# Attention and two gated layers on one core: where the reciprocals and the keys' load stand in a half

## The chip, the cores and the metric

The kernel runs on one core of a Trainium2 chip. The metric is the device time of one launch in microseconds (us); lower is better. A core has five engines that run their own instruction streams: PE (TensorE, matmuls), DVE (VectorE), ACT (ScalarE), POOL (GpSimd) and SP (SyncE, which here only issues DMAs). Each takes its instructions in program order and waits on semaphores.

## The reference

Attention over 4 batches and 8 heads of 1152 tokens with 64 channels, the queries averaged in pairs of tokens, and then two gated layers on the 2304 resulting rows of 512.

```python
q_pool = q.reshape(B, H, S // 2, 2, D).mean(axis=3)
scores = np.matmul(q_pool, k.transpose(0, 1, 3, 2)) / np.sqrt(D)
scores = scores - np.max(scores, axis=-1, keepdims=True)
attn = np.exp(scores)
attn = attn / (np.sum(attn, axis=-1, keepdims=True) + 1e-09)
x = np.matmul(attn, v)            # -> (B*S/2, H*D) rows
h = x @ w_in;  x = (h - np.tanh(h)) @ w_out
h = x @ w2_in; x = (h / (1 + np.exp(-1.702 * h))) @ w2_out
```

## The kernel before

Heads are handled in 16 pairs, `p` = 0 to 15, the two heads of a pair on the two halves of the partitions. The 576 pooled queries of a pair are cut in two, so the attention stage is a loop of 32 halves, `h` = 2p + x. [...]

A half does, for nine blocks of 128 keys, the scores (`scores`, line 429 on PE: three products and one with `row`, which subtracts the row maximum), the exponent on ScalarE (line 435), and sums of the exponents on GpSimd (line 446) and VectorE (line 464). In between, `unit` (lines 351, 359, 366) computes the plain scores of the next pair for its row maxima, which VectorE reduces (line 371). `send_rows` (lines 380 to 391) transposes the maxima on VectorE and sends them into `row` by small DMAs of SyncE: six in the odd half (part 0, before the next pair's scores start) and four in the even one (part 1; `end_rows`, line 394, finishes them). At the end of a half `products` multiplies the exponents by the values (line 480, 72 matmuls) and adds up the denominators (line 493); ScalarE copies the result out (line 501).

The order within a half is written by hand. Jobs are filed under a half and a place with `at(h, place, fn)` and run by `do(h, place)`. The places, in order: "first" and "start" (ahead of the loop over blocks and units), then after the loop "load", "pre", "gp", then `products`, then "end" and "pool". Within one place jobs run in the order in which they were filed; the weight pieces of the first gated layer are filed before the attention's own jobs.

The steps that matter here, for pair p with h = 2p:

- `sums(p - 1)`, line 514, at the start of half h: four small DMAs on SyncE bring the denominators of the previous pair into `s9`.
- `recip(p - 1)`, lines 522, 523 and 525, at the end of half h (for the last but one half at "pre"): VectorE adds three columns and takes the reciprocal `r9`, SyncE sends it to the DRAM tile `rd` (4.6 KB).
- `spread(p - 1)`, line 531, at the start of half h + 1: two DMAs on SyncE read `rd` back, broadcast over 64 partitions each, into `rbd`. They wait until `rd` has landed.
- `normalise(p - 1)`, line 540, at the end of half h + 1: VectorE multiplies the result by `rbd`.
- `load_k(p)`, line 290, at "first" of half h - 4: SyncE loads the keys into one of two buffers `kr`, whose last reader is `prep_kl` of pair p - 2 on GpSimd, at the end of half h - 5.
- `load_v(p)` (line 294, half h - 2) and `load_sum(p)` (line 285, half h - 4) at "load"; `fetch_low` (line 342) at "first" of half h - 1: further loads on SyncE.
- `load_other(p)`, line 281, at "gp" of half h - 6, and `take_qh(p)`, line 338, at "gp" of half h - 3: GpSimd issues DMAs that add to a DRAM tile, on a queue of their own.
- `prep_kh(p)`, line 321, at "pre" of half h - 3: ScalarE rounds the keys. `prep_kl(p)`, line 328, at "pool": GpSimd takes the low part; a dependency set by hand (`after`, with `last["v"]`) holds it until the VectorE instruction that `last["v"]` names is done. In an even half that was the reciprocal, in an odd one `normalise`.
- The weight pieces' conversion (`convert_steps`, lines 143, 149, 156, 163 on VectorE) runs one step in each half from half 2 on, mostly at "end", ahead of `recip`.

Of the kernel before, what the change touches and what calls it, by code (L numbers as in the profile page):

```python
# [23 lines left out]
def f32(ap):  # L24
    return ap.bitcast(F32)
# [3 lines left out]
def tile_pooled_attention_two_moe(  # L29
# [11 lines left out]
    nc = tc.nc  # L41
# [85 lines left out]
    last = {}  # L127

    def after(job, first):
        if first is not None:  # L130
            tc.add_manual_dep(job.ins, first.ins.name, mybir.DependencyInfo(
                mybir.DependencyClass.Sync, mybir.DependencyReason.DATA), reason="port")

    def convert_steps(raw, hi, lo, shape, box, eng=None):
        def shift():
            box["t"] = wpool.tile([128, DM], I32, tag="wt", name="wt", bufs=2)
            if raw.dtype == F32:
                nc.scalar.activation(f32(box["t"][:]), raw, AF.Copy)
                return
            top = raw[:, :, 1]  # L140
            box["a"] = wpool.tile([128, DM], F32, tag="wa", name="wa", bufs=1)
            nc.scalar.activation(box["a"], f32(top), AF.Abs)
            nc.vector.tensor_scalar(  # L143
                out=box["t"], in0=top, scalar1=3, scalar2=0x3FFFFFF8,
                op0=ALU.logical_shift_left, op1=ALU.bitwise_and,
            )

        def sign():
            nc.vector.scalar_tensor_tensor(  # L149
                out=box["t"], in0=raw[:, :, 1], scalar=-0x40000000, in1=box["t"],  # L150
                op0=ALU.bitwise_and, op1=ALU.bitwise_or,
            )

        def flush():
            t, a = box["t"], box["a"]
            nc.vector.scalar_tensor_tensor(
                out=f32(t[:]), in0=a, scalar=2.0 ** -15 * 1.125, in1=f32(t[:]),
                op0=ALU.is_ge, op1=ALU.mult,
            )

        def tail():
            t = box["t"]
            nc.vector.scalar_tensor_tensor(
                out=t, in0=raw[:, :, 0], scalar=29, in1=t,
                op0=ALU.logical_shift_right, op1=ALU.bitwise_or,
            )

        def split():
            t = f32(box["t"][:]).rearrange("p (a b) -> p a b", a=shape)
            nc.scalar.activation(hi, t, AF.Copy)  # L170
            job = (eng or nc.gpsimd).tensor_tensor(lo, t, f32(hi), op=ALU.subtract)  # L171
            if eng is None:
                after(job, last.pop("rest", None))

        def nothing():
            pass

        bits = [sign, flush, tail] if raw.dtype == I32 else [nothing] * 3
        return [shift, *bits, split]

# [38 lines left out]
    def attention(ctx: ExitStack):  # L219
# [19 lines left out]
        rows = [ap.tile([128, SP], F32R, name=f"row{i}") for i in range(2)]  # L239
# [152 lines left out]
        def end_rows(p):  # L392
            d = pairs[p]
            nc.vector.tensor_reduce(
                d["row"][:, 512:], f32(d["cr"][:]).rearrange("p (h i) -> p i h", h=2),
                AX.X, ALU.min)
# [17 lines left out]
        def scores(g, some=slice(0, 4)):  # L414
            p, i = divmod(g, 2 * KT)
            x, t = divmod(i, KT)
            d = pairs[p]
            sc = opened.pop(g, None)
            if sc is None:
                sc = ps.tile([128, 2, 512], F32, tag="ps", name="sc")  # L420
            else:
                some = slice(3, 4)
            ks, xs = slice(128 * t, 128 * t + 128), slice(HB * x, HB * x + HB)
            steps = (
                (d["kh"][:, ks], d["qh"]), (d["kl"][:, ks], d["qh"]),
                (d["kh"][:, ks], d["ql"]), (sel, d["row"]))
            for n, (w, m) in list(enumerate(steps))[some]:
                for s, r in enumerate(sides):
                    nc.tensor.matmul(  # L429
                        sc[:, s, 0:HB], w[r], m[r, xs], start=(n == 0), stop=(n == 3))  # L430
            if some.stop < 4:
                opened[g] = sc
                return
            pf = ap.tile([128, 2, HB], F32, tag="pf", name="pf", bufs=10)
            nc.scalar.activation(pf, sc[:, :, 0:HB], AF.Exp, scale=SCALE)  # L435
            probs[g] = pf
# [13 lines left out]
        def full(p, x):  # L450
            return 1 < 2 * p + x < 2 * NPAIR - 1

        def rest_of(p, x):
            return ((5, 6, 7, 8),) if full(p, x) else ((5, 6), (7, 8))
# [13 lines left out]
        def add_two(p, x, t):  # L468
            two = [probs[(2 * p + x) * KT + i] for i in (t - 1, t)]
            pairs[p]["twos"].append(ap.tile([128, 2, HB], F32, tag=f"two{t}", name="two"))  # L470
            nc.vector.tensor_add(pairs[p]["twos"][-1], *two)
# [74 lines left out]
        def at(h, when, fn, *args):  # L546
            jobs.setdefault((h, when), []).append(lambda: fn(*args))

        def do(h, when):
            for job in jobs.pop((h, when), ()):  # L550
                job()
# [3 lines left out]
        NH = 2 * NPAIR  # L555
# [32 lines left out]
        for p in range(NPAIR):  # L588
            h = 2 * p
            if p > 0:  # L590
                at(h - 2, "load", load_v, p)
                if p == 1:
                    at(h - 2, "pre", prep_corner, p)
                    at(h - 2, "end", prep_ql, p)
                    at(h - 2, "pool", prep_kl, p, 0)
                    at(h - 1, "end", prep_kl, p, 1, nc.vector)
                else:
                    at(h - 2, "pool", prep_kl, p, 0)
                    at(h - 1, "pool", prep_kl, p, 1)
                    at(h - 1, "first", fetch_low, p, "ql")  # L600
                at(h, "start", sums, p - 1)
                at(h, "pre" if h == NH - 2 else "end", recip, p - 1)
                at(h + 1, "start", spread, p - 1)
                at(h + 1, "end", normalise, p - 1)
            if p > 1:
                at(h - 4, "start", new_pair, p)
                at(max(h - 6, 0), "start", load_one, p)
                at(max(h - 6, 0), "gp" if p > 2 else "start", load_other, p)
                at(h - 4, "load", load_sum, p)
                at(h - 4, "first", load_k, p)  # L610
                at(h - 3, "pre", prep_qh, p)
                at(h - 3, "pre", prep_corner, p)
                at(h - 3, "pre", minus_qh, p)
                at(h - 3, "pre", prep_kh, p, 0)
                at(h - 3, "pre", prep_kh, p, 1)
                at(h - 3, "gp", take_qh, p)
# [13 lines left out]
        first, second = slice(0, 128), (slice(128, 2 * 128), slice(2 * 128, 3 * 128))  # L630
# [37 lines left out]
        for h in range(NH):  # L668
            p, x = divmod(h, 2)
            do(h, "first")  # L670
            do(h, "start")
            g = h * KT
            t = 0
            late = [t for g in rest_of(p, x) for t in g[1:]] if h < NH - 1 else []
            for u in todo[h]:
                if u is None:
                    scores(g + t)
                    if h < NH - 1 and t < KADD - full(p, x) or t < 4:
                        add(p, x, t)
                    elif h == NH - 1 and t in (5, 7):  # L680
                        add_two(p, x, t)
                    t += 1
                    if t == KT and late and h != 1:
                        add_rest(p, x, late.pop(0))
                    continue
                unit(*u)
                if u == (p + 1, 6):
                    max_rows(p + 1, 0)
                    send_rows(p + 1, 0)
                if u == (p, 10):  # L690
                    max_rows(p, 1)
                    send_rows(p, 1)
                if t == KT and late:
                    add_rest(p, x, late.pop(0))
                    if late and x == 0 and full(p, x):
                        add_rest(p, x, late.pop(0))
                        end_rows(p)
            while late:
                add_rest(p, x, late.pop(0))
            if h == NH - 2:  # L700
                end_rows(p)
            do(h, "load")
            do(h, "pre")
            do(h, "gp")
            products(p, x)
            if x == 0 and not full(p, x):
                end_rows(p)
            do(h, "end")
            do(h, "pool")
# [652 lines left out]
```

## Time and profile before

| | us |
|---|---|
| median of 3 runs | 1172.92 |
| lowest and highest | 1171.52, 1174.12 |
| the profiled execution | 1176.05 |
| its span, first to last instruction | 1174.3 |
| attention stage, about | 0 to 395 |
| PE busy in the span | 1161.6 (99%) |
| DVE, ACT, POOL busy | 992.5, 652.9, 453.6 |
| DMA moved | 156.29 MB |

The page gives the share of the span in which each engine had an instruction at work. PE's matmuls are pipelined and their ends are modelled, so its 99% says that it hardly ever stood still, not that it was at its peak. The granted clock of PE is listed per stretch; 1.00 is full speed, 2.4 GHz, and 0.50 is 1.2 GHz. A DMA's issue is a SyncE instruction of some 0.3 to 0.6 us; its landing comes later and is known through those who wait for it.

### The profile page before, as it was taken

How to read it: one execution, taken by the hardware profiler on the slowest of the kernel's cores; microseconds unless marked ns; L12 is line 12 of the kernel's file. 1: busy time of each engine (PE TensorE's matmuls, PEld its weight loads, DVE VectorE, ACT ScalarE, POOL GpSimd, SP SyncE). 2: the span in 40 equal slices, each digit the busy share in tenths (PEclk: the TensorE clock that was granted, in tenths of full speed). 3: DMA queues.
4: the chain of work that ended last, by engine and by line, in shares of the span. 5: the costliest groups of instructions: out<-in, count | busy, mean ns of one | idle time of the engine just before them, and what ended most of it. 6: DMA issues, size and time to landing. Idle time of an engine off the chain costs nothing.

```text
span 1174.3 us, 23203 instructions
## 1 busy us (share of the span) xinstructions
PE 1161.6 (99%) x9260; PEld 971.5 (83%) x9260; DVE 992.5 (85%) x1242; ACT 652.9 (56%) x969; POOL 453.6 (39%) x321
## 2 busy tenths in 40 slices
PE   9999999999999999999999999999999999999998
PEld 7767676767777888888898898898889999999996
DVE  6888988878988799999999999998986899886442
ACT  4667566656665678676666666655654333342220
POOL 7667676766766223333232333221000222222211
PEclk9999999999999999999999999999999999999999
DMA  6455655555542021111111111112998757765512
GB/s 191 123 118 137 162 127 133 146 143 130 125 111 62 12 64 36 55 54 37 54 36 54 37 36 36 37 54 95 389 389 311 275 215 287 269 225 206 206 54 90
DMA packets 58221, 156.29 MB, mean 133 GB/s; under 512 B 14080, under 2 KB 19712, under 8 KB 58112
## 3 DMA queue, kind: packets, MB, share of 16 engines
q1 hardware_dynamic: 53536, 146.14, 35.8%
q0 software_dynamic: 4032, 8.26, 4.9%
q8 instruction: 73, 1.20, 0.4%
q10 hardware_dynamic: 544, 0.39, 0.1%
q14 instruction: 36, 0.29, 0.1%
HBM read 124.39 MB, written 33.69 MB: 135 GB/s over the span
## 4 chain that ended last, share of the span: by engine, by line
PE 77%; DVE 14%; ACT 4%; issue 2%; DMA 1%; POOL 1%; SPq 1%; DVEq 0%; ACTq 0%; POOLq 0%
PE sc L429 13%; PE y L1048 13%; PE y L1236 12%; PE h L1139 11%; PE acc L480 11%; PE b L996 5%; PE a L996 3%; PE c L996 3%; PE mx L359 3%; DVE work L1182 2%; DVE work L1199 2%; DVE wt L149 2%; DVE wt L143 1%; ACT work L1180 1%; PE acc L493 1%
## 5 line engine op out<-in xcount | busy, mean ns | idle before, releaser
L371 DVE TENSOR_REDUCE mt<-mx 128x2 fp32r<-128x1024 f32 (+2 forms) x176 | 198.1, 1136 | 41.0 <-PE mx L359 22.1
L435 ACT ACTIVATE pf<-sc 128x576 f32<-128x576 f32 x288 | 173.8, 655 | 24.2 <-PE sc L429 15.1
L1236 PE MATMUL y<-mem,big 128*128 128x512 f32 (+1 forms) x780 | 185.1, 368 | 1.2 <-POOL mem L1153 1.2
L1236 PEld LDWEIGHTS y<-mem,big 128*128 128x128 f32 x780 | 142.6, 188 | 21.2 <-POOL mem L1153 2.3
L1034 POOL TENSOR_TENSOR mem<-work,mem 128x768 fp32r<-128x768 f32 x24 | 46.2, 1938 | 289.4 <-ACT mem L1029 274.4
L446 POOL TENSOR_TENSOR sum<-sum,pf 128x576 f32<-128x576 f32 x95 | 137.4, 1446 | 29.2 <-DVE rest L464 23.9
L480 PE MATMUL acc<-pf,v 128*32 128x288 f32 x2304 | 146.3, 407 | 0.0
L1139 PE MATMUL h<-mem,big 128*128 128x512 f32 (+1 forms) x564 | 127.1, 377 | 0.0
L480 PEld LDWEIGHTS acc<-pf,v 128*32 128x32 f32 x2304 | 71.6, 110 | 65.6 <-ACT pf L435 5.0
L1139 PEld LDWEIGHTS h<-mem,big 128*128 128x128 f32 x564 | 104.4, 188 | 17.0
L1153 POOL TENSOR_TENSOR mem<-work,mem 128x1024 fp32r<-128x1024 f32 (+1 forms) x40 | 89.1, 2227 | 75.9 <-ACT mem L1151 75.9
L1048 PE MATMUL y<-big,mem 128*128 128x512 f32 x405 | 114.0, 390 | 0.0
L1201 ACT ACTIVATE work<-work 128x1024 f32<-128x1024 f32 (+1 forms) x40 | 39.1, 977 | 107.5 <-DVE work L1199 107.5
L429 PE MATMUL sc<-qh,kh 64*128 64x288 f32 x576 | 94.0, 315 | 0.0
L171 POOL TENSOR_TENSOR big<-wt,big 128x512 fp32r<-128x512 f32 x25 | 32.6, 1302 | 155.5 <-ACT big L170 142.5
L429 PE MATMUL sc<-row,sel 64*128 64x288 f32 x576 | 88.5, 293 | 3.9 <-DMA row<-tt 2.4
L1048 PEld LDWEIGHTS y<-big,mem 128*128 128x128 f32 x405 | 76.0, 188 | 15.5
L429 PE MATMUL sc<-qh,kl 64*128 64x288 f32 x576 | 87.5, 293 | 0.0
L429 PE MATMUL sc<-ql,kh 64*128 64x288 f32 x576 | 87.2, 292 | 0.0
L1139 PE MATMUL h<-mem,w 128*128 128x512 f32 (+1 forms) x376 | 84.7, 377 | 0.0
L501 ACT ACTIVATE u<-acc 128x576 f32<-128x576 f32 x30 | 19.6, 653 | 107.3 <-PE acc L493 107.3
L1139 PEld LDWEIGHTS h<-mem,w 128*128 128x128 f32 x376 | 69.6, 188 | 11.3
(176 smaller groups left out, 2580.5 us busy)
## 6 DMA issues: line engine op xcount, KB each, us to landing
mem<-x SPq DMA_DIRECT2D x36, 768.0 KB
big<-x SPq DMA_DIRECT2D x27, 768.0 KB
raw<-in_moe_w_in_dram SPq DMA_DIRECT2D x32, 512.0 KB
raw<-in_moe_w_out_dram SPq DMA_DIRECT2D x32, 512.0 KB
v<-in_v_dram SPq DMA_DIRECT2D x16, 576.0 KB
x<-big SPq DMA_DIRECT2D x12, 768.0 KB
kr<-in_k_dram SPq DMA_DIRECT2D x15, 576.0 KB
rbd<-rd SPq DMA_DIRECT2D x32, 144.0 KB
```

The lines of the kernel that those rows point to most:

```text
L371: nc.vector.tensor_reduce(out, src, AX.X, ALU.max, negate=True)
L429: nc.tensor.matmul(sc[:, s, 0:HB], w[r], m[r, xs], start=(n == 0), stop=(n == 3))
L435: nc.scalar.activation(pf, sc[:, :, 0:HB], AF.Exp, scale=SCALE)
L446: job = nc.gpsimd.tensor_add(out, parts[p, x], new)
L480: nc.tensor.matmul(acc[32 * n:32 * n + 32, 0], pairs[p]["v"][:, s, t, 32 * h:32 * h + 32], new[t][:, s, :], start=(t == 0), stop=(t == KT ...
L996: nc.tensor.matmul(bank[nm][:, fp, 0:G], w[:, wo, a, 128 * c:128 * c + 128], x[:, b, c, :], start=(k == 0), stop=(k == 5))
L1034: eng.tensor_tensor(g[:, :, 1], halves[n][:, fp], f32(g[:, :, 0]), op=ALU.subtract)
L1048: nc.tensor.matmul(y, gts[2 * side + fp][:, j, r, 128 * t:128 * t + 128], wo[:, p, :], start=(k == 0), stop=(k == len(terms) - 1))
L1139: nc.tensor.matmul(hb[:, j, 0:TBS[b]], wi[:, c, w, :], x[r][c], start=(k == 0), stop=(k == 3 * NKC - 1))
L1153: eng.tensor_tensor(gt[:, :, 1, :], g, f32(gt[:, :, 0, :]), op=ALU.subtract)
L1201: nc.scalar.activation(a, u, AF.Relu, bias=-T2)
L1236: nc.tensor.matmul(ys[m][:, 0:w], lhsT, rhs, start=(fp == 0 and not low and j == p == 0), stop=(fp == 1 and low and j == 1))
```

## The change

`recip` moves from the half's end (behind the loads, the value products and the conversion step) to a new place "rows" inside the loop of the even half, right behind `end_rows`; the place runs in halves 2 to 28. So its two VectorE instructions stand ahead of the half's last row maximum, and its DMA stands ahead of the loads filed under "load". `load_k` moves from "first" to "load" of the same half, where it comes behind the values and the sums of q. The four VectorE conversion steps now set `last["v"]`, so in an even half GpSimd's low part waits for the conversion step instead of the reciprocal. Neither the count of instructions nor that of DMAs changes.

```diff
@@ convert_steps @@
-            nc.vector.tensor_scalar(
+            last["v"] = nc.vector.tensor_scalar(
                 out=box["t"], in0=top, scalar1=3, scalar2=0x3FFFFFF8,
...
-            nc.vector.scalar_tensor_tensor(
+            last["v"] = nc.vector.scalar_tensor_tensor(
                 out=box["t"], in0=raw[:, :, 1], scalar=-0x40000000, in1=box["t"],
...
@@ attention @@
                 at(h, "start", sums, p - 1)
-                at(h, "pre" if h == NH - 2 else "end", recip, p - 1)
+                at(h, "pre" if h == NH - 2 else "rows", recip, p - 1)
                 at(h + 1, "start", spread, p - 1)
...
                 at(h - 4, "load", load_sum, p)
-                at(h - 4, "first", load_k, p)
+                at(h - 4, "load", load_k, p)
...
                         add_rest(p, x, late.pop(0))
                         end_rows(p)
+                        do(h, "rows")
```

The other two conversion steps (`flush`, `tail`) are changed as the two that are shown.

## Rows read from the trace of the kernel before

**Rows 1.** the page's first part: busy time of each engine

```profile
PE 1161.6 (99%) x9260; PEld 971.5 (83%) x9260; DVE 992.5 (85%) x1242; ACT 652.9 (56%) x969; POOL 453.6 (39%) x321
```

**Rows 2.** chain that ended last: start us, us, what; line 480

```profile
70.05 4.50 PE acc L480 x72
94.73 4.50 PE acc L480 x72
...
164.50 4.50 PE acc L480 x72
188.41 4.50 PE acc L480 x72
...
211.72 4.50 PE acc L480 x72
234.93 4.50 PE acc L480 x72
261.77 4.50 PE acc L480 x72
```

**Rows 3.** waits of PE, 41 to 395 us: total us, times, longest

```profile
PE sc L429 <- DMA row<-tt: 2.0, 2, 1.6
PE sc L429 <- issue: 1.2, 1, 1.2
```

**Rows 4.** windows: stretch; busy us of five engines; PEclk, DMA share, GB/s

```profile
253.60:258.20 4.60, 4.52 (x41) 4.52 (x43) 1.93 (x5) 2.15 (x4) 1.54 (x2) 0.63 0.50 142
```

**Rows 5.** waits of SyncE's own queue, 41 to 395 us

```profile
SPq L290 <- POOL kl L328: 43.7, 12, 4.6
SPq L531 <- DMA rd<-r: 33.5, 15, 4.6
```

**Rows 6.** timeline of SyncE, halves 18 and 19: start us, us, instruction

```profile
237.06 0.38 SPq L294 DMA_DIRECT2D v<-in_v_dram  x1
...
240.76 0.33 SPq L525 DMA_DIRECT2D rd<-r  x1
...
246.21 2.15 SPq L531 DMA_DIRECT2D rbd<-rd  x2
248.45 3.29 SPq L388 DMA_DIRECT2D row<-tt  x6
```

**Rows 7.** timeline of SyncE, half 17

```profile
222.57 3.29 SPq L388 DMA_DIRECT2D row<-tt  x6
```

**Rows 8.** timeline of GpSimd, halves 18 and 19

```profile
240.04 0.83 POOL L281 DMA_DIRECT2D qd<-in_q_dram  x1
...
249.19 0.90 POOL L338 DMA_DIRECT2D qd<-qs  x1
```

**Rows 9.** line 281, 239 to 242 us: its DMA to landing

```profile
DMA to landing us min/median/max: 6.0/6.0/6.0
```

**Rows 10.** timeline of VectorE, end of half 18

```profile
238.80 1.21 DVE L371 TENSOR_REDUCE mt<-mx 128x2 fp32r<-128x1024 f32 x1
...
240.31 0.18 DVE L522 TENSOR_REDUCE r<-s 128x9 f32<-128x27 f32 x1
240.52 0.21 DVE L523 RECIPROCAL r<-r 128x9 f32<-128x9 f32 x1
```

**Rows 11.** timeline of PE's weight loads, start of half 19

```profile
240.48 0.19 PEld L429 LDWEIGHTS sc<-qh,kh 64*128 64x128 f32 x2
```

**Rows 12.** timeline of ScalarE, half 19; brackets: idle before, releaser

```profile
248.31 1.24 ACT L321 ACTIVATE kh<-kr 128x576 fp32r<-128x576 f32 x2
251.57 0.65 ACT L501 ACTIVATE u<-acc 128x576 f32<-128x576 f32 x1 [2.01 <-PE acc L493]
```

**Rows 13.** windows as in rows 4: program's start, and half 18

```profile
12.00:14.00 2.00, 2.00 (x30) 1.81 (x26) 1.88 (x3) 0.00 (x0) 0.00 (x1) 1.00 1.02 400
...
238.00:242.00 4.00, 4.00 (x60) 2.81 (x54) 3.78 (x7) 2.02 (x4) 3.18 (x3) 1.00 0.90 226
```

**Rows 14.** timeline of PE, start of half 20

```profile
253.68 0.57 PE L429 MATMUL sc<-row,sel 64*128 64x288 f32 x2 [1.59 <-DMA row<-tt]
```

More of the change, by code (lines that the diff above doesn't have):

```diff
@@ L155, in flush @@
             t, a = box["t"], box["a"]
-            nc.vector.scalar_tensor_tensor(
+            last["v"] = nc.vector.scalar_tensor_tensor(
                 out=f32(t[:]), in0=a, scalar=2.0 ** -15 * 1.125, in1=f32(t[:]),
@@ L162, in tail @@
             t = box["t"]
-            nc.vector.scalar_tensor_tensor(
+            last["v"] = nc.vector.scalar_tensor_tensor(
                 out=t, in0=raw[:, :, 0], scalar=29, in1=t,
```

## Prediction

> **What bounds the kernel now.** I read the page first: PE is busy for 1161.6 of 1174.3 us [rows 1], so only two things can move the time, an idle stretch of PE or a stretch in which its matmuls run slower. The change lies in the attention stage, so next I read the chain of waits there, and on it the start of each half's value products (line 480). Ten of the 13 pairs of halves from half 2 to 28 take 23.2 to 23.3 us, as half 16 to half 18: 234.93 - 211.72 = 23.21 [rows 2]. Three are longer: half 4 to 6 takes 24.68 (1.47 more), half 12 to 14 takes 23.91 (0.70 more), half 18 to 20 takes 26.84 (3.63 more) [rows 2]. Together that is **5.8 us**. The list of waits names what PE stood still for between 41 and 395 us: twice the maxima row (line 388's DMA, `row<-tt`), 2.0 us in all with 1.6 the longest, and once 1.2 us that the profile can't name [rows 3]; the 1.2 us stand at the same place of a half, and I count them to the same cause. The rest of the 5.8 us is slower work: in 253.60 to 258.20, right after the 1.6 us idle, the granted clock is 0.63 of full speed [rows 4], so part of that stretch ran at 1.2 instead of 2.4 GHz.
>
> Third, who makes the row late? The view of SyncE's own waits: the keys' load (line 290) stands for GpSimd's low part 43.7 us in all, and `spread` (line 531) for the landing of the reciprocals in DRAM 33.5 us, 15 times, 4.6 at the longest [rows 5]. SyncE takes its instructions in order, and the six row DMAs of an odd half stand behind `spread`. Half 18 and 19 show it: values' load at 237.06, reciprocals sent only at 240.76, spread at 246.21, rows from 248.45 on [rows 6]. Two halves earlier the rows went out at 222.57 [rows 7], which is 245.78 with 23.21 added: half 19's rows were 2.7 us late. What held the reciprocals: GpSimd had issued an accumulating DMA (line 281) at 240.04 [rows 8], and it landed 6.0 us later, at 246.0 [rows 9]; the spread was let go 0.2 us after that. A few kilobytes sent 0.7 us after the accumulate landed with it.
>
> **The change part by part.** *Reciprocals earlier (halves 2 to 28, 14 times).* VectorE makes them right behind `end_rows`, before the half's last maximum: in half 18 that maximum starts at 238.80, the reduce takes 0.18 and the reciprocal 0.21 us [rows 10], so 0.4 us later, at about 239.2, r9 is there, and its DMA leaves at about 239.3 instead of 240.76. That is ahead of the accumulate at 240.04. How long it takes to land the trace shows only beside accumulates: a mean wait of 33.5/15 = 2.2 us, at most 4.6 and, from issue to spread, 5.5 [rows 5, 6]. So the spread goes between 241.5 and 244.8; I take 242, as nothing else is then in front of it. Even the late end lies before 245.8, when the rows are ready. The rows then leave on time, and PE, which stood 1.6 us for rows that were 2.7 us late, does not wait. On the odd halves that were no later than 222.57's pattern nothing changes. Gain: 1.47 + 0.70 + 3.63 = 5.8 us of the profiled execution.
>
> *The reciprocal's cost on VectorE* is nothing by sum (the same two instructions leave the place behind the conversion step), but the half's last maximum ends 0.4 us later, at 240.4 instead of 240.01 [rows 10]. That maximum frees the PSUM tile which the second scores of the next half take; their weights are loaded at 240.48 [rows 11]. So 0.47 us of cover for 0.4: I take 0; the other end, 0.1 us in each of 14 halves, is 1.4 us.
>
> *Bulk loads behind the reciprocals.* SyncE now stands until 239.2 for r9, and the values' load goes at 239.7 instead of 237.06, 2.7 us later; the sums of q, then the keys (moved), then q's low part follow, and spread behind them. Values serve products two halves on: hidden. The keys were issued first in the half and now last in it. They are read by ScalarE (line 321) at 248.31, and ScalarE is idle 2.01 us behind it before it copies the result at 251.57 [rows 12]; so keys that land by 250.3 cost nothing. When do they land? By their shapes 576 (v) + 288 (q sums) + 576 (k) + 288 (q low) + 2 x 144 (spread) KB, 2.06 MB, now leave in one go from about 239.7, on wire from about 240.8. With full queues the DMA engines moved 400 GB/s, and around 240 us 226 GB/s [rows 13]: 5.2 to 9.1 us, so the end lies between 246 and 250; the accumulate takes engines as well, and I add an estimate of 2 us in five halves (248 to 252). I take 249, nearer to the full queue, because the lower rate is that of single loads with gaps. Keys, ahead of q's low part and spread, are there by 247: hidden. Normalise reads spread's result only behind half 19's products, as ScalarE's copy at 251.57 does [rows 12]: hidden too.
>
> *Keys' load no longer first.* The 43.7 us in which SyncE stood for GpSimd there [rows 5] go; behind it stood the sums' four DMAs, a q load and the second rows. PE never stood for those in halves that were on time [rows 2, 3], so this gains 0. For pair 2 (half 0) the load moves from the start of the program to half 0's end, still a half before its use: 0.
>
> *GpSimd's low part* waited for the reciprocal, which stood behind the conversion step; now the conversion step comes last, at the same time (0.4 us of reciprocal moved from behind it to ahead of it): 0.
>
> **A rule to weigh.** In rows, the reciprocals that were issued 0.7 us behind an accumulate of another queue landed with it [rows 6, 8, 9]. The Trainium skill's page "DMA: Bandwidth & Descriptors", section "Queues, rings and completion order", says the same for a reason: a DMA's semaphore increment is a strongly ordered write, which lands only after every earlier write of that DMA engine, whatever queue it came from. The trace agrees here. That rule also speaks against this change: six small rows issued behind 2.06 MB would be told as landed only once the bulk is written. By it rows are ready when the bulk is, and the forecast holds if that is before PE asks; if not, it is the first rival.
>
> **The rivals.** *1, slower: the rows wait behind the bulk.* Keys' load adds 576 KB in front of the rows in every odd half. In half 20 PE began on the row at 253.68, having stood 1.6 us [rows 14]: it wants it at about 252.1, and the last of the six row DMAs would be issued by 249.1 (3.3 us from 245.8 [rows 6]). It decides where the bulk ends after 252, the late end above; then the rows also run into the accumulate that GpSimd issues at 249.19 (line 338) [rows 8]. It would strike the rows of the five halves (7, 11, 15, 19, 23) behind one in which GpSimd has a weight piece's split to do ahead of the accumulate, at 1.2 to 3.6 us each (half 6's idle; half 20's with the clock): 6 to 18 us, less the 5.8 gained, so 0 to 12 slower than now, in the middle **1179**. For it: 226 GB/s at 238 to 242. Against: the start of the program keeps 400 GB/s with the same loads queued. *2, within: the gain is there but small.* The profiled execution took 1176.05 us (1174.3 span, 1.75 around it), 3.1 above the median of 1172.92. If the slow clock of half 20 happened in the profiled execution alone, the other runs hold some 5.8 - 3.1 = 2.7 us of late rows, and one of 1.2 us may stay: 1172.92 - 2.7 + 1.2 = **1171.4**. *3, within: VectorE's last maximum, 0.4 us later, holds PE* (above): 1.4 us back, **1170.9**. *4: the change doesn't do what it says*, if the sums' DMAs were not landed when VectorE comes to `recip` in the half; VectorE didn't stand before it at 240.31 [rows 10], and the sums now leave earlier, so this gets no chance of its own.
>
> **How the numbers follow.** The profiled execution would go from 1176.05 to 1170.25. For the median there are two ends: 1170.25, if its 3.1 us of difference are part of the 5.8, and 1172.92 - 5.8 = 1167.1, if all runs hold the 5.8. I take **1169.5**, nearer to the first, because the clock's drop (about 2 us) is the kind of thing that one run has and another hasn't. Chances: forecast 0.50, rival 2 0.27, rival 3 0.06, rival 1 0.17. Range 1167.0 to 1174.5: it holds the forecast, both small rivals and a mild form of rival 1. About 0.2% (2.3 us) is what a measurement of this kernel can tell from no change: faster 0.50, same 0.33, slower 0.17.
>
> **What would show it.** Right: reciprocals sent about 4.4 us after the products' start (5.8 now), spread within 7 to 8.5 us of it for all pairs (up to 11.3 now), the odd halves' rows always leaving at about 10.8, no PE wait for `row<-tt` behind half 3, all pairs of halves near 23.2 us. Wrong: rows that leave on time and land late (rival 1), PE's weights waiting on line 371 at the second scores (rival 3), `kh<-kr` on ScalarE waiting for the keys, or long pairs of halves at other places.

## The result, and the profile after

| | us | runs |
|---|---|---|
| before, beside the runs of after | 1172.22 (1170.20 to 1175.01) | 6 |
| after | 1179.37 (1177.49 to 1182.10) | 6 |
| ratio after to before | 1.0062, 95% interval 1.0041 to 1.0082 | |
| profiled execution of after, and its span | 1181.01, 1179.2 | |

The change makes the kernel 7.2 us slower, where 3.4 us faster was predicted. The profiled execution of after is 4.96 us longer than that of before (1176.05).

The first part of the page says little, as [rows 1] did: PE is busy 0.7 us longer than before and the span is 4.9 us longer, so PE stands still more.

```profile
PE 1162.3 (99%) x9260; PEld 971.2 (82%) x9260; DVE 992.1 (84%) x1242; ACT 653.4 (55%) x969; POOL 452.8 (38%) x321
```

**Where.** The chain that ended last, starts of line 480 in the even halves 4 to 20 (columns as in [rows 2]):

```profile
71.22 4.50 PE acc L480 x72
96.11 4.50 PE acc L480 x72
...
121.46 4.50 PE acc L480 x72
...
144.63 4.50 PE acc L480 x72
169.53 4.50 PE acc L480 x72
194.46 4.51 PE acc L480 x72
218.34 4.50 PE acc L480 x72
...
241.52 4.50 PE acc L480 x72
...
265.07 4.50 PE acc L480 x72
```

In [rows 2] three of 13 pairs of halves were long. Here only 8 to 10 (23.17) and 16 to 18 (23.18) of these eight have the old length; the others take 24.89, 25.35, 24.90, 24.93, 23.88 and 23.55. With 2 to 4 (24.93) and 22 to 24 (25.01), eight of the 13 pairs are long. Over 23.25 each, that is 197.44 - 8 x 23.25 = **11.4 us**, where before had 5.8. Take it away and 1181.0 - 11.4 = 1169.6 is left; before gave 1176.05 - 5.8 = 1170.25. So the whole loss is in these pairs, and both kernels have the same floor of about 1170 us.

**What PE waited for**, 41 to 395 us (total us, times, longest, as [rows 3]):

```profile
PE sc L429 <- DMA row<-tt: 5.7, 8, 1.4
PE sc L429 <- issue: 2.0, 2, 1.7
```

It is the maxima row again: 7.7 us in ten waits, against 3.2 in three. (The waits put down to "issue" are waits for the row too: the one of 1.7 us ends at 115.12, and the semaphores' events in the trace tell the sixth row DMA of that half as landed at 115.03.) The other 3.7 of the 11.4 us were not divided further; the granted clock of the whole run is 1.0, so no long stretch ran slow, as half 20 did in [rows 4].

**What SyncE waited for**, in the same stretch, to lay beside [rows 5]:

```profile
SPq L525 <- DVE r L523: 74.2, 14, 5.7
...
SPq L388 <- DMA kr<-in_k_dram: 9.1, 9, 1.7
SPq L531 <- DMA rd<-r: 6.8, 9, 1.2
SPq L388 <- DMA ql<-qd: 6.4, 12, 1.5
```

The third line is the gain: `spread` stood 33.5 us for the reciprocals' landing and now stands 6.8. The first is its price: SyncE stands 14 times, 5.7 us at the longest, for the reciprocal, and now with all the bulk loads behind it; the kernel before stood there too (56.0 us), but its values, q sums and keys had gone ahead. The second and fourth are new: the row's DMAs (line 388) stand, before they are even issued, for the landing of the **keys** and of **q's low part** (what is left of the queries when they are rounded), whose data they do not touch. Of that kind the same view of before holds one row, a single wait of 2.0 us near the attention's start. It stands second here, behind before's wait for the reciprocal:

```profile
SPq L525 <- DVE r L523: 56.0, 14, 6.7
...
SPq L388 <- DMA kr<-in_k_dram: 2.0, 1, 2.0
```

**One half in full.** The timeline of SyncE at the end of half 4 and in half 5 (value products of half 4 start at 71.22), to lay beside [rows 6]:

```profile
75.58 0.33 SPq L525 DMA_DIRECT2D rd<-r  x1
76.01 0.37 SPq L294 DMA_DIRECT2D v<-in_v_dram  x1
76.51 0.35 SPq L285 DMA_DIRECT2D qs<-qd  x1
76.97 0.40 SPq L290 DMA_DIRECT2D kr<-in_k_dram  x1
77.89 0.33 SPq L342 DMA_DIRECT2D ql<-qd  x1
78.95 1.15 SPq L531 DMA_DIRECT2D rbd<-rd  x2
81.86 5.26 SPq L388 DMA_DIRECT2D row<-tt  x6
```

The six row DMAs take 5.26 us to issue, where [rows 6, 7] show 3.29. Count back eight DMAs from the fifth: four rows, two spreads, q's low part, keys. Eight back from the sixth is q's low part. The trace lists the semaphores of each DMA of SyncE: eight are signalled in turn, and the fifth row DMA waits on the one that the keys' DMA signals, the sixth on that of q's low part. So, as this program is built, a DMA is issued only when the one eight places ahead of it has landed; e6 tests whether these waits are what costs.

By then it is too late for another reason. GpSimd's accumulating DMA, and the last row matmul that waits in half 6 on PE (brackets as in [rows 14]):

```profile
85.37 0.90 POOL L338 DMA_DIRECT2D qd<-qs  x1
...
89.77 0.37 PE L429 MATMUL sc<-row,sel 64*128 64x288 f32 x1 [0.86 <-DMA row<-tt]
```

The last rows, when they leave behind the accumulate, land 2.1 to 3.3 us after their issue ends, where a row on its own takes 1.0. PE wants them about 17 us after the products' start and goes on at 89.77, 18.5 us after it. This tells long pairs from short ones: in the eight long pairs the sixth row lands 17.2 to 19.0 us after the products' start, in the other five 15.4 to 15.9.

The first four rows are issued in time, but they land late as well: in half 5 they are told as landed at 85.7 to 86.2, 2.1 to 3.2 us after their issue, and the keys that left before them at 85.6. So their data do queue behind the bulk, as the prediction's first rival had it. In no half, though, does a fourth row land later than 16.2 us after the products' start, before PE asks, and four of the five pairs of the old length have the same delay at no cost.

When do the keys land? Windows of half 5 (columns as in [rows 4]):

```profile
79.50:81.50 2.00, 2.00 (x36) 1.92 (x32) 1.97 (x3) 1.59 (x4) 1.92 (x2) 1.00 0.85 305
81.50:83.50 2.00, 2.00 (x31) 1.36 (x32) 1.82 (x4) 1.88 (x4) 1.54 (x2) 1.00 1.00 372
83.50:85.50 2.00, 2.00 (x40) 1.05 (x33) 2.00 (x3) 1.06 (x3) 1.49 (x2) 1.00 0.49 123
```

Most of the bulk moves at 305 to 372 GB/s, but the last 2 us bring 123, with the DMA engines busy 0.49 of the time. The keys are told as landed at about 85.6, 14.5 us after the products' start (12.8 to 14.8 over the halves). ScalarE waits for them too (41 to 400 us), which it never did before:

```profile
ACT kh L321 <- DMA kr<-in_k_dram: 4.9, 6, 1.2
```

### The profile page after: what moved, and what is told of

Read it like the earlier page. It is cut to its first block, busy times and chain, and to the rows that moved or that the text cites. A ratio compares the mean times of both kernels' runs of the same rounds, so it can differ in the third digit from the quotient of the medians.

```text
span 1179.2 us, 23215 instructions
## 1 busy us (share of the span) xinstructions
PE 1162.3 (99%) x9260; PEld 971.2 (82%) x9260; DVE 992.1 (84%) x1242; ACT 653.4 (55%) x969; POOL 452.8 (38%) x321
## 4 chain that ended last, share of the span: by engine, by line
PE 73%; DVE 12%; DMA 6%; ACT 3%; issue 3%; SPq 1%; POOL 1%; DVEq 0%; ACTq 0%; POOLq 0%
PE y L1237 13%; PE y L1049 12%; PE h L1140 12%; PE sc L429 10%; PE acc L480 9%; PE b L997 5%; DMA ql<-qd 4%; PE a L997 3%; PE c L997 3%; PE mx L359 2%; DMA row<-tt 2%; DVE work L1200 2%; DVE work L1183 2%; DVE wt L143 1%; DVE wt L149 1%
## 5 line engine op out<-in xcount | busy, mean ns | idle before, releaser
L429 PE MATMUL sc<-row,sel 64*128 64x288 f32 x576 | 91.2, 293 | 8.1 <-DMA row<-tt 5.7
L1025 ACT ACTIVATE work<-work 128x768 f32<-128x768 f32 x36 | 29.5, 844 | 86.9 <-DVE work L1020 83.1
```

Of the source, the lines that this page charges most:

```text
L429: nc.tensor.matmul(sc[:, s, 0:HB], w[r], m[r, xs], start=(n == 0), stop=(n == 3))
```

## The experiments

**The theory** (A in the expectations): the bulk leaves only behind the reciprocal, 2 to 3 us later than before; the keys, now late in it, land at up to 14.8 us; the fifth and sixth row DMA may not be issued before that, miss the accumulate, and PE stands. The chief rival (C in the expectations) is that of the prediction: the rows are issued in time, and it is their data's queueing behind the bulk that costs. In the first batch the kernel before took 1174.0 us (median of 23 runs, 1170.0 to 1178.3), in the second 1174.43 (20 runs, 1171.31 to 1178.24).

**Reciprocals early, keys where they were (e1).** The change without its second part.

```diff
-                at(h - 4, "load", load_k, p)
+                at(h - 4, "first", load_k, p)
```

> The changed kernel with the keys' load put back to the head of the half; reciprocals still early. Theory A (the keys' load behind the bulk is the loss: SyncE's fifth and sixth row DMA of an odd half stand until the keys and q's low part, issued eight DMAs ahead, have landed): SyncE's waits of line 388 for kr and ql vanish, no PE wait for row<-tt behind half 3, about 1170.2 us (the lowest runs of before), 0.2% under before. Theory B (the early reciprocal itself costs: VectorE's last maximum is 0.4 us later, values and q sums leave 2.7 us later): stays at 1177 to 1180.

Measured: **1170.53 us** (1170.20 to 1171.02), ratio to before 0.9970 [0.9959, 0.9982]. PE never waits for a row; all pairs of halves take 23.2 to 23.3 us. SyncE's waits, 41 to 395 us:

```profile
SPq L290 <- POOL kl L328: 50.7, 12, 4.6
SPq L531 <- DMA rd<-r: 12.1, 10, 1.9
```

The reciprocals' part does what the prediction said: they leave 4.4 us after the products' start, `spread` stands 12.1 instead of 33.5 us and leaves at 6.0 to 8.4. In halves 6, 10, 14 and 18, where they now are ahead of line 281's accumulate (97.88 against 98.67 in half 6), spread follows them 1.8 to 2.6 us later, where it took 3.9 to 5.5 before. The keys' 50.7 us for GpSimd, which the change set out to remove, are there in full and cost nothing. The later last maximum on VectorE costs nothing either: PE's weights waited for it once, 0.2 us.

**Keys in the bulk, reciprocals late (e2).** The kernel before with the second part alone.

```diff
-                at(h - 4, "first", load_k, p)
+                at(h - 4, "load", load_k, p)
```

> The kernel before with the keys' load moved to the half's bulk loads and nothing else; reciprocals still sent behind the bulk. Theory A: at least as slow as the changed kernel, 1177 to 1183, but by another wait as well: the reciprocals now lie behind 1.47 MB, so spread leaves after 10.5 us in most odd halves and the rows leave late. Theory B: 1170 to 1173, as before.

Measured: **1173.08 us** (1172.20 to 1175.55), ratio 0.9996 [0.9984, 1.0009]. A forecast 1177 to 1183: a miss. SyncE in half 4 and 5 (products of half 4 at 70.51):

```profile
70.03 0.38 SPq L294 DMA_DIRECT2D v<-in_v_dram  x1
71.33 0.35 SPq L290 DMA_DIRECT2D kr<-in_k_dram  x1
76.59 0.33 SPq L525 DMA_DIRECT2D rd<-r  x1
...
81.40 3.28 SPq L388 DMA_DIRECT2D row<-tt  x6
```

Here the bulk does not stand behind the reciprocal: the keys leave 0.8 us after the products' start, not 5.8, land well before the rows come, and no row DMA waits for them. What A lacked was this: keys in the bulk are harmless by themselves. The late rows of the kernel before stay (PE waits of 1.8 and 0.6 us). So neither part costs anything alone (-3.5 us, and -0.9 us, which is within the interval), and together they cost 5 to 7 us.

**Keys earlier still (e3)**: at "start", behind the sums' DMAs, so that SyncE's wait for GpSimd goes as well.

```diff
-                at(h - 4, "load", load_k, p)
+                at(h - 4, "start", load_k, p)
```

> The changed kernel with the keys' load at the half's start, behind the denominators' four DMAs, so that it stands neither for GpSimd at the head nor in the bulk. Theory A: as the kernel with the keys first, about 1170.2; SyncE's 43.7 us for GpSimd's low part are gone and that is worth nothing. Theory B: 1177 to 1180.

Measured: **1170.09 us** (1169.78 to 1170.82), ratio 0.9967 [0.9955, 0.9979]. It beats both kernels. The waits for GpSimd's low part are gone, and that is worth nothing that can be told from e1 (0.4 us).

**Accumulate out of the rows' way (e4).** After, with GpSimd's line 338 moved behind the half's products.

```diff
-                at(h - 3, "gp", take_qh, p)
+                at(h - 3, "pool", take_qh, p)
```

> The changed kernel with GpSimd's accumulating DMA of the odd halves (line 338) issued behind its low part of the keys, some 4 us later, so that late rows are not behind it. Theory A: the rows leave as late as in the changed kernel (up to 15.5 us after the products' start), but land 1.1 us later instead of 2.5 to 3.3; PE's waits of 7.7 us fall to 1 to 2 and the time to about 1172. Theory C (the engines are full of bulk and the rows land late whatever runs beside them): 1177 to 1180.

Measured: **1176.14 us** (1175.25 to 1178.01), ratio 1.0017 [1.0009, 1.0026]. Waits of PE's matmuls, of its weight loads, and of SyncE:

```profile
PE sc L429 <- DMA row<-tt: 0.5, 2, 0.3
...
PEld sc L429 <- DVE mt L371: 3.3, 11, 0.3
...
SPq L388 <- DMA kr<-in_k_dram: 9.5, 10, 1.7
```

Half hit, half miss. The row DMAs still stand for the keys (9.5 us) and leave as late as 17.2 us after the products' start, but the sixth lands 1.0 to 1.4 us after its issue ends, and PE's waits for them fall from 7.7 to 1.0 us (0.5 here, and 0.5 that the profile can't name). So the accumulate is the second link of the chain. The time is 4 us above what was expected, since something new came: most pairs take about 23.5 us (189.75 to 213.29: 23.54), and PE's weights wait 11 times, 3.3 us in all, for VectorE's last maximum, once in after. GpSimd now issues the accumulate (0.9 us) behind its low part; how that slows VectorE was not followed further.

**Bulk first again, reciprocals early (e5).** After, with the bulk issued ahead of the new place.

```diff
+                        do(h, "load")
                         do(h, "rows")
```

> The changed kernel with the half's loads (values, q sums, keys) issued just ahead of the early reciprocals instead of behind them, so that they do not stand for r9. Theory A' (neither part costs by itself: the keys in the bulk are late only since the bulk is held until r9 is there, 4.4 us after the products' start, 2.6 us later than without): SyncE's row DMAs no longer stand for kr or ql, the reciprocals land behind the bulk, 1170.5 to 1173.5. Rival (the order of the small DMA and the bulk does not matter, the pair of edits costs in another way): 1177 to 1181.

Measured: **1170.23 us** (1169.79 to 1171.32), ratio 0.9965 [0.9953, 0.9978], 0.3 us under what A' expected; PE waits for no row. SyncE (products at 69.95):

```profile
70.46 0.35 SPq L290 DMA_DIRECT2D kr<-in_k_dram  x1
74.33 0.33 SPq L525 DMA_DIRECT2D rd<-r  x1
77.81 1.52 SPq L531 DMA_DIRECT2D rbd<-rd  x2
80.59 3.29 SPq L388 DMA_DIRECT2D row<-tt  x6
```

The same DMAs with the same bytes as after, in another order, and the loss is gone: it is not the amount of data, nor the place in the count alone (the keys stand eight places ahead of the fourth row here), but that the bulk leaves 5.2 us earlier in the half and the keys have landed by then (6.0 to 8.4 us after the products' start). Nor need the reciprocals be ahead of the bulk: with the keys before them they still land by 5.9 to 9.4 us after the products' start, ahead of the rows.

**Four DMAs of 16 bytes (e6).** After, with four tiny loads behind `spread` in the odd halves; they do no work for the result.

```diff
+                for i in range(4):
+                    nc.sync.dma_start(out=tiny[0:1, 4 * i:4 * i + 4],
+                                      in_=q[0, 0][0:1, 0, 0:4])
```

> The changed kernel with four more DMAs of 16 bytes each on SyncE between spread and the six row DMAs of an odd half; they do no work for the result. They are issued in the 2 us in which SyncE would wait for the rows anyway. Theory A (a DMA of SyncE stands for the landing of the DMA eight places ahead): now the first row DMA stands eight places behind the keys' load, so all six leave after 14 us instead of two of them; PE waits some 2.5 us more in ten to thirteen halves, 1200 to 1215. Theory C (the rows wait in the DMA engines behind the bulk, not for their issue): no change, 1177 to 1182.

Measured: **1210.23 us** (1208.14 to 1214.68), ratio 1.0308 [1.0275, 1.0342]. They move 64 bytes a pair and cost 31 us; some of it is the clock, which fell to 0.96 on the mean of 41 to 420 us behind PE's longer stands. SyncE's waits, 41 to 420 us (helper lines are one higher here; 535 is the tiny DMA, 389 the row's), and PE's:

```profile
SPq L389 <- DMA kr<-in_k_dram: 29.9, 13, 4.5
SPq L535 <- DMA qs<-qd: 9.6, 13, 2.0
SPq L535 <- DMA v<-in_v_dram: 8.3, 11, 2.3
SPq L389 <- DMA ql<-qd: 5.8, 10, 1.4
SPq L389 <- DMA rbd<-rd: 1.5, 2, 0.8
...
PE sc L430 <- DMA row<-tt: 22.9, 14, 2.6
```

Each pair is eight places apart: third tiny and v, fourth and q's sums, first row and keys, second row and q's low part, third row and the first spread. A hit for A. SyncE's stands come before the issue, where data queueing behind data cannot be the reason: a row of 512 bytes waits for 576 KB of keys because of its place in the count, and it waits in 13 halves where it waited in 9.

**Keys on GpSimd's queue (e7).** After, with the keys' DMA issued by GpSimd, so that it takes no place in SyncE's count.

```diff
-            return nc.sync.dma_start(out=kraw[p][:, x], in_=k[p // NPB, p % NPB][:, x])
+            queue = nc.sync if p < 2 else nc.gpsimd
+            return queue.dma_start(out=kraw[p][:, x], in_=k[p // NPB, p % NPB][:, x])
```

> The changed kernel with the keys' load of pairs 2 to 15 issued at the same place by GpSimd, on the other queue: the same bytes at about the same time, but out of SyncE's row of DMAs. Theory A: no row DMA stands for kr any more, at most for ql; 1170 to 1174. Theory C: the same bytes fill the same engines, 1177 to 1182.

Measured: **1169.72 us** (1168.96 to 1171.06), ratio 0.9959 [0.9945, 0.9974], the fastest of all and 0.3 us under what A expected. The waits for row and for landings eight places ahead that are left (lines are one higher here too):

```profile
PE sc L430 <- DMA row<-tt: 0.4, 1, 0.4
...
SPq L389 <- DMA ql<-qd: 0.2, 1, 0.2
```

The keys' DMA on GpSimd, in half 4 (products at 69.53):

```profile
71.78 0.59 POOL L291 DMA_DIRECT2D kr<-in_k_dram  x1
```

The loss is gone, but this run does not part the count from the time. GpSimd does not stand for the reciprocal, so the keys leave 2.3 us after the products' start instead of 5.8, not "at about the same time" as the expectation had it, and land at 6.2 to 8.1. Either could take the rows' wait away (e5 shows it for the time); that the place in the count matters by itself rests on e6.

**The third part of the change (e8).** e3 with the four `last["v"] =` of the conversion steps taken out, so that GpSimd's low part no longer waits for them.

```diff
-            last["v"] = nc.vector.tensor_scalar(
+            nc.vector.tensor_scalar(
```

> The kernel with early reciprocals and the keys' load at the half's start (1170.1), with the third part of the change undone: in an even half GpSimd's low part depends on the reciprocal, which is now early, and may run beside VectorE's conversion step. If that dependency is worth nothing: 1169.8 to 1170.6. If the two engines slow each other: the conversion step or the low part is longer than 0.68 and 1.43 us, and the time is 1171 to 1175.

Measured: **1183.94 us** (1181.96 to 1185.79), ratio 1.0077 [1.0056, 1.0098], 13.8 us above e3 and 9 us above the upper end of what was expected. VectorE's line 143 in e3 (count, min/median/max ns, first and last start):

```profile
L143 DVE TENSOR_SCALAR wt<-raw x8: 367/416/419, 53.3 to 377.3; 128x512 int32<-128x512 int32 x8
```

The same line in e8:

```profile
L143 DVE TENSOR_SCALAR wt<-raw x8: 367/2400/3741, 52.3 to 388.8; 128x512 int32<-128x512 int32 x8
```

One of these steps in e8's timeline, with GpSimd's beside it:

```profile
196.07 3.74 DVE L143 TENSOR_SCALAR wt<-raw 128x512 int32<-128x512 int32 x1
...
196.47 1.70 POOL L328 TENSOR_TENSOR kl<-kr,kh 128x576 fp32r<-128x576 f32 x1
197.92 1.59 POOL L446 TENSOR_TENSOR sum<-pf 128x576 f32<-128x576 f32 x1
```

And a wait of PE in e8, 41 to 395 us:

```profile
PE mx L359 <- DVE mt L371: 8.2, 6, 2.9
```

A conversion step of 0.42 us takes 2.4 us at the median and 3.74 at the longest beside GpSimd: in the lines shown it begins ahead of two GpSimd operations and ends at 199.81, 0.3 us after the second (199.51). The one step in e8 with no GpSimd operation beside it is the shortest, 0.37 us. The maximum behind it is late, and PE stands 8.2 us for maxima; how the other 5.6 of the 13.8 us divide was not worked out. The Trainium skill's page "SBUF — State Buffer", section "Who interferes with whom", states that VectorE and GpSimd share a pair of ports, which one holds for a whole instruction while the other is blocked, and counts this kind of VectorE operation among those that can ask for it. The trace agrees in kind: one step lasts for as long as both GpSimd operations beside it. It does not show what the same section says of the order, that whoever issues first keeps the ports: five of the eight steps are recorded as started 0.4 us ahead of line 328 and are held all the same. Why is open.

## Why the prediction was wrong, point by point

- *Bound, and where the time lies before*: right. Late rows are where the kernel before lost its time, and a floor of about 1170 us for the profiled execution (1170.25 there) is what e1, e3, e5 and e7 reach (1170.5, 1170.1, 1170.2, 1169.7). The lower end taken for the median (1167.1) was too low: no run of any kernel came under 1168.96. The kernel before also differs more from run to run (1170.0 to 1178.3, against 0.8 to 2.1 us of spread in these four); that late rows make the difference is likely, but only one of its executions was profiled.
- *Reciprocals earlier*: right, as e1 shows, in size (3.5 us of median) and in place (sent at 4.4 us, spread at 6.0 to 8.4). In mechanism right in every second even half, where the accumulate comes late; in the others line 281's accumulate is issued about 2.2 us after the products' start, still ahead of them, and spread follows 2.9 to 4.0 us later, early enough. "The rows then leave on time" holds only where the DMAs eight places in front have landed.
- *VectorE's last maximum 0.4 us later* (rival 3): right at 0; in e1 the weights of the second scores waited for it once, 0.2 us.
- *Bulk loads behind the reciprocals*: **the step that failed.** It took the keys as there "by 247", 12.1 us after the products' start of half 18 (234.93 in [rows 2]), and the last of the six row DMAs as "issued by 249.1", as if issue were free of the bulk. A row DMA's issue stands for the DMA eight places ahead, so the fifth waits for the keys' landing and the sixth for q's low part. The one wait of 2.0 us in the view of before was the sign, and the semaphores' turn stood in its trace; the prediction used neither. SyncE stands 9.1 us for the keys and 6.4 us for q's low part, and PE 7.7 us for rows. The size failed too: the keys land 12.8 to 14.8 us after the products' start, up to 2.7 later than taken. The term "2.06 MB" at close to the full queue's rate has no slow tail, where the trace shows 123 GB/s in the last 2 us. Why the tail lags is open. The 2 us added for the accumulate in five halves rest on no row; the bulk ends at 15.2 to 16.4 us in those halves and at 14.5 to 16.3 in the others.
- *"Keys' load no longer first"*: right that the removed 43.7 us gain nothing (e1 against e3). That the moved load costs nothing is right alone (e2) and wrong beside the reciprocals' new place; with the bulk first again it is right once more (e5).
- *GpSimd's low part*: 0 was right for the change as it stands; e8 shows that the dependency guards 13.8 us.
- *Rival 1* had the place (rows in the odd halves, accumulate of line 338), the sign and the time (1179 against 1179.37), with too small a chance. Its mechanism was half right: the rows run into the accumulate, and the first four do queue as data behind the bulk, but in time for PE; the late ones are the fifth and the sixth, held at issue, in eight pairs of halves and not five. So the hit on the time is in part luck. The rule that was weighed there, on landing in order behind earlier writes, fits the first four rows, told as landed right behind the keys, and the last ones, which land 2.1 to 3.3 instead of 1.0 us after an issue behind the accumulate (in e4, without it, 1.0 to 1.4 us are left).

## What to carry to other kernels

When a load is moved on a queue whose DMAs signal on a few semaphores in turn, count that many DMAs on from its new place: what stands there is not issued before the load has landed, however small it is. Price a moved step together with the other moves: here each of two was free or a gain, and both together cost 5 to 7 us, as one held the bulk back and the other put 576 KB of keys into it, eight places ahead of an urgent row. Waits of an issuing engine that nobody stands for, as the 43.7 us here, are not worth a change.

## What the hardware showed that was not expected

- As this program is built, SyncE's DMAs are tied together by eight semaphores: four loads of 16 bytes cost 31 us of 1179 (e6), with 29.9 us of standing for keys alone. The Trainium skill's page "DMA: Bandwidth & Descriptors", section "Why a DMA increments its semaphore by 16 and not by 1", asks for one semaphore for each slot in flight; eight semaphores are then eight slots, and the waits in e6 stand exactly there.
- An accumulating DMA on GpSimd's queue holds small DMAs of SyncE that follow it: 2.1 to 3.3 us from the end of issue to landing instead of 1.0 (after; gone in e4).
- One VectorE step can be held for as long as GpSimd's operations beside it last: 3.74 us instead of 0.42 (e8).
